# Pacing the row gathers of a fused convolution and expert layer by landings and by matrix steps

## The chip, the cores and the metric

The kernel runs on one core of one Trainium2 chip. A core has five engines with an instruction queue each, which run side by side and wait for one another through semaphores: TensorE (PE; its weight loads are shown apart as PEld), VectorE (DVE), ScalarE (ACT), GpSimd (POOL) and SyncE (SP, which here only starts transfers). Sixteen DMA engines move data between the device's memory and the on-chip buffers. The metric is the device time of one execution in microseconds (us); a version counts by the median of its runs.

## The reference

Two branches act on the same normalised input and are added to it:

```python
def reference(A_q, A_k, A_v, A_shift_k, A_ssm_k, A_ssm_D, B_x, B_w_q, B_k1, B_k2, B_u, B_v):
    ...
        # A: short causal convolution of k, times v, then a long causal convolution
        kv = k_shift * v
        y = irfft(rfft(pad(kv)) * rfft(pad(ssm_k)))[:, :S] + kv * ssm_D
        return q * y
    ...
        # B: each token picks 2 of 4096 experts per head by product keys
        q = jnp.einsum("nd,dhc->nhc", xf, w_q)
        s1 = jnp.einsum("nhd,ed->nhe", q1, k1)
        s2 = jnp.einsum("nhd,ed->nhe", q2, k2)
        i1 = jnp.argsort(-s1, axis=-1)[..., :K]
        i2 = jnp.argsort(-s2, axis=-1)[..., :K]
        ...
        ue = u[top_e]
        ve = v[top_e]
        act = _gelu(jnp.einsum("nd,nhkd->nhk", xf, ue))
        out = jnp.einsum("nhk,nhk,nhkd->nd", g, act, ve)
    ...
    x = A_q
    xn = _layernorm(x, axis=-1)
    return x + _A_ref(xn, A_k, A_v, A_shift_k, A_ssm_k, A_ssm_D) + _B_ref(xn, B_w_q, B_k1, B_k2, B_u, B_v)
```

(The long convolution is written out here in short; the code does it with FFTs.) There are 2048 tokens of 448 channels, 16 heads, and two experts per head, so each token fetches 32 rows. A row of `u` and one of `v` lie side by side in one table, `uv`, and are fetched together.

## The kernel before

The tokens are cut into 16 tiles of 128. The work is a set of streams, written as Python generators that yield operations: an engine, a cost in us, a function that emits the instructions, what it waits for, and what it makes available. A planner (`Planner.run`, L190) plays a list schedule with these costs: it takes the operation that can start first by its own clock, emits its instructions, and goes on. The order of instructions on every engine is the order in which the planner emitted them, and is fixed when the kernel is built. The framework then puts a semaphore wait wherever an instruction needs data or a buffer of another one.

There are three parts in time. First the weights of the scores are folded with the keys (`w_load` to `w_low`; SP loads 16 pieces of `wq`). Then, tile after tile, the scores are made (`s_mm`, PE, L394 to L398), DVE takes the top values of each of 32 groups (`s_top`: eight `max` at L430, and eight `max_index` at L435 in four operations of two), small DVE operations (L462 to L478) choose the two experts per head, PE turns the result round (L506), and ACT writes the row numbers to `idx` and the weights to `gt` (L495). After the last tile's scores their buffers are given back, and the convolution (from `c_in`, L785, to `c_gate`, L904) runs in two halves of channels, with `fm` tables loaded by SP (L809).

The expert streams run beside all of that. A batch is a set of 4 gathers, and there are 128 batches, 512 gathers in all. A gather (L524) is one indirect DMA that POOL issues: it fetches 128 rows of 896 floats, by the row numbers in `idx`, to a quarter of a `uv` buffer. There are 5 such buffers (`NBUF`), of which one is lent to the convolution for some time; a batch takes the buffer that comes free first, so its first gather waits for the value step of the batch that had it. For a batch, PE spreads the tokens (`xr`, L537), DVE multiplies them into the rows (L557 takes two gathers at once, L564 one), ACT sums what L557 left (L576), takes the gelu (L580) and weighs it (L604; DVE at L602 for some), and PE adds up the values (`pv`, L615, the value step that frees the buffer). ACT copies the sums of a tile's quarter (`vs`, L625), PE folds them (L634) and DVE adds them to the output (L636).

POOL issues nothing but gathers, except at the start and for 14 products of the short convolution of the second half (`tap`, L676), which lie between gathers in its queue; DVE adds those at L701. A gather signals its landing on one of eight semaphores in turn, so the framework already makes each gather wait for the landing of the eighth ahead.

Of the kernel before, what the change touches and what calls it, by code (L numbers as in the profile page):

```python
# [33 lines left out]
HOLD = 11  # L34
SHIFT = 2
ON_POOL = (1, 3)


N = 2 * S
# [42 lines left out]
class Ring:  # L82


    def __init__(self, n, banks=None):
        self.n, self.releases, self.banks = n, [], banks
# [51 lines left out]
class Planner:  # L138
# [5 lines left out]
    def __init__(self):  # L144
        self.free = dict.fromkeys(("PE", "DVE", "ACT", "POOL", "SP"), 0.0)
        self.busy = dict(self.free)
        self.done, self.streams, self.dma, self.loads, self.part = {}, [], 0.0, 0.0, 0.5
        self.log = {e: [] for e in self.free}

    def add(self, prio, ops):  # L150
        s = [prio, iter(ops), None]
        self.streams.append(s)
        return s
# [33 lines left out]
    def run(self, until):  # L187
        while any(s in self.streams for s in until):
            for s in list(self.streams):
                if s[2] is None:  # L190
                    s[2] = next(s[1], None)
                    if s[2] is None:
                        self.streams.remove(s)
            heads = {}
            for s in self.streams:
                t = self.start(s[2])
                if t is not None:
                    heads.setdefault(s[2].eng, []).append((t, s[0]() if callable(s[0]) else s[0], s))
            if not heads:
                if any(s in self.streams for s in until):  # L200
                    raise RuntimeError("no operation can go on: " + str([(s[0], s[2].eng, s[2].key, s[2].waits) for s in self.streams]))
                return
            best = None
            for eng, cands in heads.items():
                cands.sort(key=lambda c: (c[0], c[1]))
                pick = cands[0]
                while True:
                    late = [c for c in cands if c[1] < pick[1] and c[0] < pick[0] + pick[2][2].cost - (self.SLIP if pick[1] < 3 else 0.0)]
                    if not late:
                        break  # L210
                    pick = min(late, key=lambda c: (c[1], c[0]))
                if best is None or pick[0] < best[0]:
                    best = pick
            t, _, s = best
            op, s[2] = s[2], None
            op.fn()
            end = t + op.cost
            self.busy[op.eng] += op.cost
            self.log[op.eng].append((t, op.cost))
            self.free[op.eng] = end  # L220
            for r, k in op.rings:
                r.releases.append(k)
                if getattr(r, "banks", None):
                    r.banks.append(k)
            if op.moved:
                end = self.transfer(op, end + 2.0) + 0.6
            if op.key is not None:
                self.done[op.key] = (end + op.lag, op.eng if not op.moved else "DMA")
# [3 lines left out]
def parallel_kernel(ctx, tc, x, wq, kk, uv, cf, cm, h0, kv0, hv1, k1, ca, out):  # L232
    nc = tc.nc
    ctx.enter_context(tc.manual_schedule())
    ap = ctx.enter_context(tc.tile_pool(name="ap", bufs=1))
# [4 lines left out]
    ws_ctx = ExitStack()  # L240
    wp = ws_ctx.enter_context(tc.tile_pool(name="wp", bufs=1))
    plan = Planner()
    r_xr, r_uv, banks = Ring(1), Slots(NBUF, plan), Slots(6, plan)
    r_sc, r_a, r_v, r_z = (Ring(n, banks) for n in CAPS)

# [14 lines left out]
    idx = ap.tile([P, NT, NG], I32, name="idx")  # L260
# [6 lines left out]
    live = {}  # L267
# [151 lines left out]
    def s_top(tiles):  # L419
        for T in tiles:  # L420
            def begin(T=T):
                live["mx", T] = wp.tile([P, 32, 8], F32, tag="mx", bufs=2, name="mx")
                live["mi", T] = wp.tile([P, 32, 8], U32, tag="mi", bufs=2, name="mi")
            for n in range(4):
                def peak(T=T, n=n):
                    live["top"] = T + n / 4
                    if n == 0:
                        begin()
                    for j in range(8):
                        nc.vector.max(live["mx", T][:, 8 * n + j, :], live["sc", T, n][:, 64 * j:64 * j + 64])  # L430
                yield Op("DVE", 1.05, peak, [("sc", T, n)], rings=[(r_mx, ("eg", T))] if n == 0 else [])
                for j in range(0, 8, 2):
                    def find(T=T, n=n, j=j):
                        for k in range(8 * n + j, 8 * n + j + 2):
                            nc.vector.max_index(live["mi", T][:, k, :], live["mx", T][:, k, :], live["sc", T, n][:, 64 * (k % 8):64 * (k % 8) + 64])  # L435
                    yield Op("DVE", 0.4, find, key=("tk", T, n) if j == 6 else None, rings=[(r_mi, ("eg", T))] if n == j == 0 else [])

# [76 lines left out]
    NB = len(order)  # L514
    ends = {(r, j): max(b for b, o in enumerate(order) if o[0] == r and o[2] == j) for r in range(len(rounds)) for j in range(4)}

    def e_gather():
        for b, (r, T, j, hf) in enumerate(order):
            for c in range(4):
                def go(b=b, T=T, g=8 * j + 4 * hf + c, c=c):  # L520
                    if c == 0:
                        live["batch"] = b
                        live["uv", b] = gp.tile([P, 4, 2 * D], F32, tag=f"uv{r_uv.first()}", name="uv")
                    nc.gpsimd.indirect_dma_start(live["uv", b][:, c, :], None, uv, bass.IndirectOffsetOnAxis(ap=idx[:, T, g:g + 1], axis=0))  # L524
                if c == 0 and loan.slot is None and ("y", 0, 0) in plan.done:
                    loan.take()
                yield Op("POOL", 1.25, go, [("idx", T, hf if T == 0 else 0)], key=("land", b, c), moved=4.6e5,
                         rings=[(r_uv, ("v", b))] if c == 0 else [])
# [156 lines left out]
    def t_taps():  # L685
        def by(b, t):
            return ("POOL", 1.1, nc.gpsimd) if t in ON_POOL else ("DVE", 0.62, nc.vector)
        for b in range(NBK):
# [232 lines left out]
    def lead():  # L921
        return -1 if live["top"] < live["batch"] / 8 + AHEAD else 2
    scores = [plan.add(p, s(range(1, NT))) for s, p in ((s_mm, lead), (s_split, lead), (s_top, lead), (s_pairs, lead), (s_gate, -1), (s_place, -1), (s_put, -1))]
    experts = [plan.add(0, s()) for s in (e_gather, e_values, e_weigh, e_share, e_spread, e_dots, e_gelu, e_out, e_fold)]
    plan.run(heads)
    f13, skd = (ap.tile([P, WS], F32, tag="ws", bufs=2, name="cs") for i in range(2))
# [79 lines left out]
```

## Time and profile before

| | us |
|---|---|
| runs | 976.0, 967.79, 976.12 (median 976.0) |
| the profiled execution, device time | 965.93 |
| its span, first to last instruction | 964.1 |
| POOL: median time to issue one gather | 0.946 |

The profiled execution had a mean granted TensorE clock of 0.866 of full speed. The page gives the busy time of each engine, the queues' bytes, the chain of work that ended last (followed back from the last instruction, at each step to what released it) and the groups of instructions by line. A group's row reads: line, engine, operation, output and inputs, count; then busy time and mean duration in ns; then the idle time of the engine just ahead of them, and what ended most of that. In a row of the timeline the first two numbers are start and duration in us, and the bracket gives the idle time ahead and its releaser. "remote", and in the chain "another core or an unknown queue", stand for a wait whose end the profile can put down to no instruction; "issue" is idle time with no releaser at all near its end.

### The profile page before, as it was taken

Reading aid. Unit: us, or ns where it says so; the run is one execution under the profiler, and the core shown is the slowest. Engines: PE = TensorE matmul, PEld = TensorE weight load, DVE = VectorE, ACT = ScalarE, POOL = GpSimd, SP = SyncE. Lnnn points to the kernel's source line nnn. Section 1 sums busy time; section 2 is a strip of 40 time slices with the busy share of each in tenths; the row PEclk is TensorE's granted clock in tenths of the full one; section 3 lists DMA queues with packets and bytes.
Section 4 is the critical chain, followed back from the end, with each engine's and each line's share of the span. In section 5 each row is a group of like instructions: output and inputs, shape, how many; then the busy total and the mean of one; then the engine's idle time right before and its main releaser. Section 6 shows DMA issues by size and latency. Waiting matters only on the chain.

```text
span 964.1 us, 16745 instructions
## 1 busy us (share of the span) xinstructions
PE 748.2 (78%) x5100; PEld 417.0 (43%) x5100; DVE 658.3 (68%) x2559; ACT 589.4 (61%) x1971; POOL 511.0 (53%) x532
## 2 busy tenths in 40 slices
PE   6948668758898798878876776788778885986886
PEld 3425333424454444434433444344436664543454
DVE  4538666867797778968868669887684751673645
ACT  4745665656675666656656757695863662874642
POOL 0063365564565666556665565667673465366530
PEclk9978787878878988879998786999997986998888
DMA  9983588796888978878888998889999588599852
GB/s 380 389 314 124 197 307 304 257 330 211 281 290 297 316 259 304 295 255 304 294 312 302 406 330 314 291 292 391 329 324 386 161 301 297 181 357 360 314 204 87
DMA packets 55338, 280.68 MB, mean 291 GB/s; under 512 B 9425, under 2 KB 13905, under 8 KB 54353
## 3 DMA queue, kind: packets, MB, share of 16 engines
q0 software_dynamic: 40960, 234.91, 69.5%
q1 hardware_dynamic: 13856, 42.43, 11.5%
q10 hardware_dynamic: 432, 2.28, 0.7%
q8 instruction: 41, 0.67, 0.3%
q14 instruction: 49, 0.39, 0.1%
HBM read 275.91 MB, written 3.67 MB: 290 GB/s over the span
## 4 chain that ended last, share of the span: by engine, by line
PE 42%; DVE 19%; ACT 14%; issue 11%; another core or an unknown queue 8%; DMA 4%; POOL 1%; DVEq 0%; ACTq 0%; SPq 0%
PE pv L615 9%; ACT uv L576 6%; DVE uv L557 6%; PE ps L785 5%; DVE mi L435 4%; PE fin L893 4%; PE psx L817 4%; DMA uv<-in_uv_dram,idx 3%; PE sc L394 3%; DVE mx L430 3%; PE psu L849 3%; PE xr L537 3%; PE sc L396 3%; PE sc L395 2%
## 5 line engine op out<-in xcount | busy, mean ns | idle before, releaser
L524 POOL DMA_INDIRECT uv<-in_uv_dram,idx x512 | 494.9, 967 | 405.4 <-issue 129.7
L576 ACT ACTIVATE uv<-uv 128x448 f32<-128x448 f32 x434 | 245.3, 568 | 69.6 <-DVE uv L557 37.2
L557 DVE TENSOR_TENSOR uv<-xr,uv 128x896 f32<-128x896 f32 x217 | 232.1, 1077 | 27.9 <-PE xr L537 15.4
L615 PE MATMUL pv<-uv,cc 128*32 128x448 f32 x1024 | 168.6, 626 | 83.4 <-ACT cc L604 31.4
L435 DVE FIND_INDEX8 mi<-mx,sc 128x8 uint32<-128x64 f32 x512 | 105.1, 219 | 11.6 <-issue 11.5
L394 PE MATMUL sc<-wh,xh 128*128 128x512 f32 x192 | 92.5, 482 | 12.4 <-ACT xh L408 9.1
L615 PEld LDWEIGHTS pv<-uv,cc 128*32 128x32 f32 x1024 | 39.3, 114 | 140.3 <-ACT cc L604 42.4
L785 PE MATMUL ps<-cs,x 128*64 128x132 f32 x896 | 75.5, 320 | 30.0 <-issue 16.7
L430 DVE MAX8 mx<-sc 128x8 f32<-128x64 f32 x512 | 73.1, 211 | 27.6 <-remote 11.9
L396 PE MATMUL sc<-wh,xl 128*128 128x512 f32 x192 | 85.2, 444 | 4.7 <-DVE xl L415 3.6
L395 PE MATMUL sc<-wl,xh 128*128 128x512 f32 x192 | 84.9, 442 | 3.1 <-issue 1.8
L785 PEld LDWEIGHTS ps<-cs,x 128*64 128x64 f32 x896 | 63.7, 160 | 53.3 <-issue 32.1
L576 ACT ACTIVATION_READ_ACCUMULATOR uv<-uv 128x1 f32 x434 | 82.2, 189 | 0.0
L625 ACT ACTIVATE vs<-pv 128x448 f32<-128x448 f32 x68 | 36.6, 538 | 68.1 <-remote 37.1
L834 DVE TENSOR_TENSOR x<-psx,x 128x448 f32<-128x448 f32 x66 | 40.9, 621 | 53.7 <-ACT x L827 38.7
L394 PEld LDWEIGHTS sc<-wh,xh 128*128 128x128 f32 x192 | 41.6, 217 | 68.2 <-issue 32.4
L604 ACT ACTIVATE cc<-fg,ge 128x32 f32<-128x32 f32 x284 | 67.7, 310 | 1.5
L795 ACT ACTIVATE x<-ps 128x396 f32<-128x396 f32 (+1 forms) x84 | 35.7, 461 | 50.9 <-remote 25.3
L849 PE MATMUL psu<-x,fm 128*128 128x224 f32 x248 | 57.2, 371 | 9.2 <-DVE x L834 4.8
L817 PE MATMUL psx<-x,fm 128*128 128x448 f32 x132 | 59.9, 583 | 2.7 <-DMA fm<-in_cm_dram 1.8
L537 PE MATMUL xr<-xn,rep 32*128 32x448 f32 x136 | 50.0, 676 | 15.4 <-DVE uv L557 8.7
L849 PEld LDWEIGHTS psu<-x,fm 128*128 128x128 f32 x248 | 46.1, 195 | 28.5 <-issue 16.5
(100 smaller groups left out, 982.8 us busy)
## 6 DMA issues: line engine op xcount, KB each, us to landing
wq<-in_wq_dram SPq DMA_DIRECT2D x16, 896.0 KB
fm<-in_cm_dram SPq DMA_DIRECT2D x32, 320.0 KB
uv<-in_uv_dram,idx POOLq DMA_INDIRECT x512
x<-in_hv_dram SPq DMA_DIRECT2D x2, 1792.0 KB
acc<-in_x_dram SPq DMA_DIRECT2D x1, 3136.0 KB
x<-in_kv_dram ACTq DMA_DIRECT2D x2, 1048.0 KB
kst<-in_k_dram SPq DMA_DIRECT2D x7, 268.0 KB
out_dram<-acc SPq DMA_DIRECT2D x1, 1344.0 KB
```

The source lines that it names most:

```text
L394: nc.tensor.matmul(sc, xh[:, c, :], wh[:, c, ns], start=(c == 0), stop=False)
L395: nc.tensor.matmul(sc, xh[:, c, :], wl[:, c, ns], start=False, stop=False)
L396: nc.tensor.matmul(sc, xl[:, c, :], wh[:, c, ns], start=False, stop=False)
L430: nc.vector.max(live["mx", T][:, 8 * n + j, :], live["sc", T, n][:, 64 * j:64 * j + 64])
L435: nc.vector.max_index(live["mi", T][:, k, :], live["mx", T][:, k, :], live["sc", T, n][:, 64 * (k % 8):64 * (k % 8) + 64])
L524: nc.gpsimd.indirect_dma_start(live["uv", b][:, c, :], None, uv, bass.IndirectOffsetOnAxis(ap=idx[:, T, g:g + 1], axis=0))
L557: nc.vector.tensor_mul(u, live["xr", r, j][:, None, :D].broadcast_to([P, 2, D]), u)
L576: nc.scalar.activation(u, u, AF.Copy, accum_out=live["act", b][:, c:c + 1])
L615: nc.tensor.matmul(pv[32 * c:32 * c + 32, :D], cc[:, c, :], buf[:, c, D:], start=first, stop=last, tile_position=(0, 32 * c))
L785: nc.tensor.matmul(ps[64 * i:64 * i + 64, w * j:w * j + w], src, f1[:, i, :], start=True, stop=True, tile_position=(0, 64 * i))
L817: nc.tensor.matmul(ps[:, :2 * HALF], live["fm", g, q // 2][:, q % 2, :128], x1[:, :, :, q, :], start=True, stop=True)
L849: nc.tensor.matmul(o, fm[:, k, at:at + 128], y, start=(j == 0), stop=(j == 1))
```

## The change

Two waits are added to gathers, and one order is turned round.

1. From the fifth gather on, each waits for the landing of the fourth ahead of it (`FLY`).
2. The planner keeps a list of its PE steps: the planned end of each and its last instruction. When a gather is planned at `plan.now`, the last step with a planned end of at least 1.5 us earlier (`BEHIND`) is looked up among the last 40, and the gather waits for it, unless the gather named last had the same one.
3. In `s_top`, the searches for the indices of a group of eight go from its last member to its first. The operations, their costs and their places in the plan stay.

```diff
+FLY = 4
+BEHIND = 1.5
+DATA = mybir.DependencyInfo(mybir.DependencyClass.Sync, mybir.DependencyReason.DATA)
...
+        self.now, self.steps, self.last = 0.0, [], None
...
             op, s[2] = s[2], None
+            self.now = t
             op.fn()
             end = t + op.cost
+            if op.eng == "PE":
+                self.steps.append((end, self.last()))
...
     plan = Planner()
+    plan.last = lambda: nc.cur_bb.bb.instructions[-1].name
...
                     def find(T=T, n=n, j=j):
-                        for k in range(8 * n + j, 8 * n + j + 2):
+                        for k in range(8 * n + 7 - j, 8 * n + 5 - j, -1):
                             nc.vector.max_index(live["mi", T][:, k, :], live["mx", T][:, k, :], live["sc", T, n][:, 64 * (k % 8):64 * (k % 8) + 64])
...
+    landed = []
+
     def e_gather():
...
-                    nc.gpsimd.indirect_dma_start(live["uv", b][:, c, :], None, uv, bass.IndirectOffsetOnAxis(ap=idx[:, T, g:g + 1], axis=0))
+                    it = nc.gpsimd.indirect_dma_start(live["uv", b][:, c, :], None, uv, bass.IndirectOffsetOnAxis(ap=idx[:, T, g:g + 1], axis=0))
+                    if len(landed) >= FLY:
+                        tc.add_manual_dep(it.ins, landed[-FLY].ins.name, DATA, reason="gathers on their way")
+                    landed.append(it)
+                    gate = next((name for end, name in reversed(plan.steps[-40:]) if end <= plan.now - BEHIND), None)
+                    if gate is not None and gate != live.get("gate"):
+                        live["gate"] = gate
+                        tc.add_manual_dep(it.ins, gate, DATA, reason="gathers keep step with PE")
```

## The prediction

> **What bounds the kernel now.** I read the page first (busy shares, queues, the chain that ended last), then that chain stage by stage, then two stretches of the timeline.
>
> ```profile
> span 964.1 us, 16745 instructions
> PE 748.2 (78%) x5100; PEld 417.0 (43%) x5100; DVE 658.3 (68%) x2559; ACT 589.4 (61%) x1971; POOL 511.0 (53%) x532
> q0 software_dynamic: 40960, 234.91, 69.5%
> PE 42%; DVE 19%; ACT 14%; issue 11%; another core or an unknown queue 8%; DMA 4%; POOL 1%; DVEq 0%; ACTq 0%; SPq 0%
> L524 POOL DMA_INDIRECT uv<-in_uv_dram,idx x512 | 494.9, 967 | 405.4 <-issue 129.7 <-ACT gt L495 46.4 <-DVE mx L430 45.6
> ```
>
> No engine is full. The gathers move 234.91 MB in 512 calls, 459 KB each, and the chain hardly ever waits for them (DMA 4%). What stands out is 8% "another core or an unknown queue": there is only one core, so these are waits for which the profile finds no releaser just before the wait ended. By stage:
>
> ```profile
> by line: another core or an unknown queue 17.1%; PE pw L346 10.9%; DVE mi L435 9.3%; DVE mx L430 7.4%; issue 6.5%; ACT xn L296 6.3%; DMA wq<-in_wq_dram 4.4%; DVE uv L557 3.9%; DMA uv<-in_uv_dram,idx 3.9%; ACT uv L576 3.7%; PE pt L323 3.3%;
> by line: another core or an unknown queue 11.8%; PE pv L615 10.1%; ACT uv L576 9.8%; PE sc L394 8.3%; DVE uv L557 8.1%; issue 7.8%; PE sc L396 6.7%; PE sc L395 6.4%; DVE mi L435 6.1%; DVE mx L430 4.4%; PE xr L537 4.2%; PE sc L398 3.4%; ACT
> by line: issue 11.7%; ACT uv L576 9.6%; DVE uv L557 9.1%; PE pv L615 9.0%; DMA uv<-in_uv_dram,idx 7.9%; another core or an unknown queue 7.3%; PE ps L785 5.8%; DVE mi L435 4.3%; POOL uv L524 3.9%; DVE tap L676 3.5%; DVE tap L751 2.9%; ACT c
> by line: issue 14.9%; PE fin L893 12.6%; PE ps L785 11.8%; PE psx L817 10.8%; PE pv L615 10.7%; PE psu L849 8.6%; PE psz L873 5.2%; another core or an unknown queue 3.7%; PE xr L537 3.1%; DMA uv<-in_uv_dram,idx 2.1%; DVE x L834 2.0%; ACT uv
> ```
>
> The four rows are the chain in 0 to 136 us, 136 to 425, 425 to 660 and 660 to 964. The unexplained share is 17.1% of 136 = 23 us, 11.8% of 289 = 34 us, 7.3% of 235 = 17 us, 3.7% of 304 = 11 us: 85 us in all. The timeline shows what they are (rows of POOL, PE, DVE and ACT, in order of time):
>
> ```profile
> 119.12 0.94 POOL L524 DMA_INDIRECT uv<-in_uv_dram,idx  x1 [3.49 <-ACT ge L580]
> 124.12 0.50 PE L398 MATMUL sc<-wr,xl 64*128 64x512 f32 x1
> 126.73 0.95 POOL L524 DMA_INDIRECT uv<-in_uv_dram,idx  x1 [0.30 <-issue]
> 127.98 0.95 POOL L524 DMA_INDIRECT uv<-in_uv_dram,idx  x1 [0.30 <-issue]
> 132.99 0.95 POOL L524 DMA_INDIRECT uv<-in_uv_dram,idx  x1 [0.30 <-issue]
> 133.38 1.15 DVE L430 MAX8 mx<-sc 128x8 f32<-128x64 f32 x8 [7.84 <-remote]
> 136.42 0.54 ACT L625 ACTIVATE vs<-pv 128x448 f32<-128x448 f32 x1 [6.37 <-remote]
> ```
>
> POOL issues 12 gathers one behind the other, one per 1.25 us (126.73 to 127.98), which asks for 459 KB / 1.25 = 367 GB/s. The score step that ended at 124.62 is seen by DVE at 133.38, 8.8 us later, with DVE free for 7.84 us of it. ACT sees an earlier value step at 136.42 after 6.37 us idle. So the signal of a finished PE step is held while a burst runs, and comes about when the burst's last gather (132.99 + 0.95 = 133.94) is done. A full DMA alone does not do it:
>
> ```profile
> 8.00:40.00 32.00, 30.81 (x149) 14.58 (x146) 15.79 (x86) 18.73 (x56) 0.00 (x0) 1.00 1.01 422
> 124.00:136.00 12.00, 6.21 (x25) 3.18 (x24) 3.01 (x15) 5.67 (x22) 7.57 (x8) 1.00 0.97 354
> ```
>
> (Columns: stretch, its length, busy of PE, PE loads, DVE, ACT, POOL, clock, DMA share, GB/s.) From 8 to 40 us SP's weight loads fill the DMA at 422 GB/s and PE is busy 30.81 of 32 us; in the burst 354 GB/s of gathers leave PE 6.21 of 12 us.
>
> **The gates on PE steps.** In the plan (which the change leaves as it is: no cost, order or due time is touched) each gather has a last PE step that ends at least 1.5 us ahead of it. I laid that list over this execution. From 136 to 425 us 163 of 180 gathers start before their step has ended, by 3.6 us on the mean over all 180; from 425 to 660 it is 34 of 142, and before 136 us 5 of 44. One burst:
>
> ```profile
> 224.59 0.94 POOL L524 DMA_INDIRECT uv<-in_uv_dram,idx  x1 [9.04 <-DVE mi L435]
> 227.19 0.96 PE L615 MATMUL pv<-uv,cc 128*32 128x448 f32 x8
> 231.02 0.96 PE L615 MATMUL pv<-uv,cc 128*32 128x448 f32 x8
> 233.58 0.95 POOL L524 DMA_INDIRECT uv<-in_uv_dram,idx  x1 [0.30 <-issue]
> 236.01 1.15 DVE L430 MAX8 mx<-sc 128x8 f32<-128x64 f32 x8 [3.40 <-PE px L323]
> 238.47 2.34 PE L615 MATMUL pv<-uv,cc 128*32 128x448 f32 x8 [2.96 <-ACT cc L604]
> ```
>
> These eight gathers run in 9.0 us (224.59 to 233.58). Gated, the first waits for the value step that ends at 228.15 (227.19 + 0.96), the fourth for 231.98, the eighth for 240.81: over 12.6 us, 1.6 us each, or 287 GB/s asked for instead of 367. That burst would not fill the DMA, and DVE's 3.40 us would mostly go. I take 65% of the 34 us of this stage: 22 us. Where the steps have ended in time, as at 119 us, the gate still works once a signal is held: the gather at 127.98 has the score step of 124.62 as its gate, whose signal came at 133.38. It and the four behind it would stop, the burst would end at 127.68 instead of 133.94, and by the distance seen (burst end to release 2.5 us at most: 133.94 to 136.42) all is free by 130.2, 3.2 us of 8.8 earlier. I take 35% of the other stages: 0.35 x (23 + 17 + 11) = 18 us. Bounds for both: nothing, and all 85 us.
>
> What waits behind a gated gather is POOL's own queue: later gathers, and 14 tap products. The users of the gathers are DVE's products (two gathers each, x99 to 400 us):
>
> ```profile
> 0.00:400.00 400.00, 197.93 (x208) 0.85 0.81 285
> 0.00:400.00 400.00, 104.92 (x99) 0.85 0.81 285
> 136.00:425.00 289.00, 170.95 (x180) 0.83 0.84 287
> L701 DVE TENSOR_TENSOR ksh<-ksh,tap 128x512 f32<-128x512 f32 x21 | 16.3, 776 | 3.1 <-POOL tap L676 2.6
> L524 POOLq EVENT_SEMAPHORE  x179: 17/43/11349, 22.5 to 919.4; - x179
> L476 DVE TENSOR_TENSOR eg<-sl,epair 128x16 f32<-128x16 f32 (+1 forms) x17 | 3.0, 174 | 3.2 <-DVE sl L475 2.8
> ```
>
> At 400 us 208 gathers have been issued (first row, POOL L524) and 2 x 99 = 198 used (second row, DVE L557): 10 ahead. At the stage's pace (third row, L524) of 289 us / 180 = 1.61 us that is 16 us of lead. A landing takes 3.7 to 6.4 us (below), so 10 us of cover remain against a delay of 3.6 us: no cost. Without that cover every late microsecond would reach DVE. The taps: DVE already waits 2.6 us for them in all; if each of the 14 is held as long as a gather is on the mean, 3.6 us, that is 50 us at the very most, but most are planned well ahead of their sums, so I take 2 us.
>
> **The landing of the fourth ahead.** Pieces of the chain that run from a gather to its landing, and L524 in three stretches:
>
> ```profile
> 503.06 3.68 DMA uv<-in_uv_dram,idx
> 649.15 6.36 DMA uv<-in_uv_dram,idx
> 709.42 6.30 DMA uv<-in_uv_dram,idx
> 600.00:700.00 100.00, 58.25 (x60) 0.93 0.91 323
> 425.00:660.00 235.00, 139.35 (x142) 0.87 0.88 312
> 660.00:964.00 304.00, 142.52 (x146) 0.88 0.78 282
> ```
>
> A piece runs from the start of the issue, so a gather is on its way 3.7 to 6.4 us, at 1.25 us each three to five together. Four on their way feed one per 0.92 to 1.59 us. From 600 to 700 us 60 gathers go out, one per 1.67 us. So this wait trims bursts only where other loads stretch the landing; I take nothing either way (ends: the whole 11 us after 660 us as a gain, the first rival as a loss).
>
> **Added waits.** A wait that an instruction cannot carry costs POOL's sequencer 43 ns (the semaphore row's median). Some 355 gates change from one gather to the next: 15 us in the queue, hidden by the 405.4 us that POOL idles ahead of gathers; exposed, they cost 15 us. PE, SP and ACT get no new instruction, and no queue's order changes.
>
> **The index searches.** 64 groups of eight: the first search now needs the maximum written just before it. An operation that waits for the one before it loses 3.2 / 17 = 0.19 us (L476's idle time): at most 12 us on DVE, whose chain share is 19%, so 2 us. The seven behind need no wait of their own any more; a gain is bounded by the same 12 us. I take 2 us of cost.
>
> **Sum.** The profiled execution took 965.93 us for a span of 964.1. 965.9 - 22 - 18 + 2 + 2 = 930. The shown runs have a median of 976.0 and reach down to 967.79, so the profiled one lies at their fast end; I keep 930 for the median, 4.7% below 976.0.
>
> **Rivals.**
> Late gathers (slower). After 425 us the limit of four becomes the pace, since POOL now also waits out each landing before it starts the next. If a gather is on its way 7.3 us, 0.95 us (its issue, L524's rows) beyond the longest piece seen, four give one per 1.83 us where 1.67 is used; over the 288 gathers issued after 425 us (142 + 146) that is 46 us, and the gate's 22 us before remain: 966 + 46 - 22 = 990. It decides from 4 x 1.67 = 6.7 us on the mean. For it: 6.36 and 6.30 us beside SP's loads. Against: fewer gathers queued should shorten just that. The Trainium skill, "DMA: Bandwidth & Descriptors", section "Anatomy of one DMA — SWDGE (gpsimd) path", puts such a DMA at some 2.0 us plus its bytes at 436 GB/s, by an estimate 3.05 us for a gather; by it four would give one per 0.76 us and this rival could not be. The trace's 3.68 to 6.36 us do not agree. Chance 0.11.
>
> POOL's work itself holds the others, not its burst (no change). The gathers' 494.9 us on POOL stay, however they are spaced, and the stalls move with them: 965.9 + 4 = 970. For it: DVE stalls too while POOL runs. Against: ACT at 136.42 is held just as long, and the release follows the burst's end. The Trainium skill, "GPSIMD Engine Reference", section "1. Specifications", says that GpSimd shares its SBUF interfaces with VectorE; by that rule alone DVE would suffer, and ACT's row speaks against it. Also here: the gates do not bind as executed, because a faster PE runs ahead of POOL. Chance 0.15.
>
> Nearly all held signals go (much faster). 965.9 - 85 + 4 = 885, since the feedback stops each burst at its start. For it: between bursts signals come at once. Against: the first burst of a stage still has open gates. Chance 0.15.
>
> **Chances and range.** 0.59 for the forecast, whose own range is 905 to 955; 0.15, 0.15 and 0.11 for the others. A measurement of this kernel tells about 1% from no change. Faster by more: 0.59 + 0.15 = 0.74; within: 0.15; slower: 0.11. The range runs from 890, near the all-gone case, to 972, past the no-change case; what is left out is the late-gather case and a little beyond.
>
> **What would show it.** Right: unexplained waits fall from 8% of the chain to about 4.5%, most between 136 and 425 us; gathers in the timeline start 1.5 us or more apart there, with PE as their releaser; GB/s is more even; DVE waits for gather landings no more than now. Wrong: the unexplained share stays (second rival), or DVE's products wait for landings and POOL's idle time ahead of L524 is released by DMA (first rival).

## The result, and the profile after

Four runs of the changed kernel took 929.56 to 935.89 us, median 933.71; the kernel before, timed beside it, had a median of 976.06 us. The ratio is 0.959 (95% interval 0.9537 to 0.9644): 4.1% faster. The profiled execution took 935.89 us.

The page after: span, busy shares and the chain by engine.

```profile
span 934.1 us, 16999 instructions
PE 741.5 (79%) x5100; PEld 411.8 (44%) x5100; DVE 665.9 (71%) x2559; ACT 590.1 (63%) x1971; POOL 511.3 (55%) x532
PE 38%; DVE 17%; DMA 14%; issue 11%; ACT 10%; another core or an unknown queue 7%; POOL 2%; SPq 0%; DVEq 0%; POOLq 0%; ACTq 0%
```

The same work in 30 us less. The unexplained waits are down only from 8% to 7%, and DMA is up from 4% to 14%: one wait went, another came. The chain in 0 to 136, 136 to 425, 425 to 660 and 660 to 934 us (one chain, followed back from the last instruction and cut into stages) tells where:

```profile
by line: another core or an unknown queue 22.1%; DMA acc<-in_x_dram 17.9%; PE pv L632 6.3%; DVE mi L443 6.2%; DVE uv L574 5.3%; DVE mx L438 4.7%; DMA wq<-in_wq_dram 4.5%; ACT uv L593 3.7%; issue 3.6%; DMA uv<-in_uv_dram,idx 3.5%; PE xr L554
by line: issue 11.0%; PE pv L632 10.5%; DMA uv<-in_uv_dram,idx 9.7%; another core or an unknown queue 8.9%; ACT uv L593 8.6%; DVE uv L574 7.2%; PE sc L402 6.7%; PE sc L404 5.3%; PE sc L403 5.2%; DVE mi L443 4.9%; PE sc L406 3.3%; POOL uv L5
by line: issue 13.8%; PE ps L802 11.2%; DVE uv L574 9.2%; PE pv L632 7.9%; ACT uv L593 6.9%; another core or an unknown queue 5.6%; PE psx L834 4.8%; DVE mi L443 4.3%; DVE mx L438 3.2%; DMA fm<-in_cm_dram 3.0%; PE psu L866 2.9%; DVE tap L69
by line: DMA uv<-in_uv_dram,idx 20.4%; issue 11.5%; PE fin L910 11.2%; PE ps L802 7.3%; PE pv L632 7.2%; PE psu L866 7.1%; PE psx L834 6.4%; PE psz L890 5.1%; POOL uv L534 3.1%; ACT uv L593 2.2%; DVE uv L574 2.0%; PE xr L554 1.7%; DVE ksh L
```

In the first stage 28.29 us of the unexplained share are one piece at 31.95 us, while weights load, where the chain of before ran through PE's folding. Such a piece comes and goes with the path that the chain takes there, so a share of the chain has to be read with care. From 136 us on the unexplained share fell from 11.8% of 289 us to 8.9% and from 7.3% of 235 us to 5.6%, and in the last stage it is no longer among the shown lines. But landings of gathers (`DMA uv`) now hold 9.7% of the second stage (28 us) and 20.4% of the last (56 us), which had 2.1% before.

The timeline of POOL at the place where the prediction showed a burst:

```profile
120.38 0.94 POOL L534 DMA_INDIRECT uv<-in_uv_dram,idx  x1 [0.54 <-issue]
122.35 0.94 POOL L534 DMA_INDIRECT uv<-in_uv_dram,idx  x1 [1.03 <-ACT cc L621]
...
128.39 0.94 POOL L534 DMA_INDIRECT uv<-in_uv_dram,idx  x1 [1.15 <-ACT uv L593]
...
134.55 0.94 POOL L534 DMA_INDIRECT uv<-in_uv_dram,idx  x1 [1.20 <-DVE uv L574]
136.35 0.94 POOL L534 DMA_INDIRECT uv<-in_uv_dram,idx  x1 [0.85 <-issue]
137.59 0.95 POOL L534 DMA_INDIRECT uv<-in_uv_dram,idx  x1 [0.30 <-issue]
138.85 0.95 POOL L534 DMA_INDIRECT uv<-in_uv_dram,idx  x1 [0.30 <-issue]
```

Thirteen gathers start between 120.38 and 138.85 us, one per 1.54 us instead of 1.25, with short waits spread among them. The other side is the view of POOL's waits (in all, times, longest), before:

```profile
POOL uv L524 <- DMA uv<-in_uv_dram,idx: 6.1, 6, 2.2
```

and after, followed by DVE's products of before and of after:

```profile
POOL uv L534 <- DMA uv<-in_uv_dram,idx: 64.2, 59, 3.7
POOL uv L534 <- PE pv L632: 27.4, 26, 3.9
```

```profile
L557 DVE TENSOR_TENSOR uv<-xr,uv 128x896 f32<-128x896 f32 x217 | 232.1, 1077 | 27.9 <-PE xr L537 15.4 <-remote 6.4 <-issue 3.6
```

```profile
L574 DVE TENSOR_TENSOR uv<-xr,uv 128x896 f32<-128x896 f32 x217 | 232.9, 1080 | 48.9 <-DMA uv<-in_uv_dram,idx 27.6 <-PE xr L554 9.4 <-remote 5.1
```

POOL waits 64.2 us for landings, ten times as long as before, and DVE's products 27.6 us, which they hardly did before. DVE also waits longer for the `tap` products of POOL, which stand in one queue with the gathers: 2.6 us in all before (the `ksh` row in the prediction), and now

```profile
DVE ksh L718 <- POOL tap L693: 15.5, 5, 4.2
```

So two effects of opposite sign lie in the 4.1%.

### The profile page after: what moved, and what is told of

Its sections match the earlier page's. It is cut to its first block, busy times and chain, and to the rows that moved or that the text cites. A ratio compares the mean times of both kernels' runs of the same rounds, so it can differ in the third digit from the quotient of the medians.

```text
span 934.1 us, 16999 instructions
## 1 busy us (share of the span) xinstructions
PE 741.5 (79%) x5100; PEld 411.8 (44%) x5100; DVE 665.9 (71%) x2559; ACT 590.1 (63%) x1971; POOL 511.3 (55%) x532
## 4 chain that ended last, share of the span: by engine, by line
PE 38%; DVE 17%; DMA 14%; issue 11%; ACT 10%; another core or an unknown queue 7%; POOL 2%; SPq 0%; DVEq 0%; POOLq 0%; ACTq 0%
DMA uv<-in_uv_dram,idx 10%; PE pv L632 8%; DVE uv L574 6%; ACT uv L593 6%; PE ps L802 5%; DVE mi L443 4%; PE fin L910 3%; PE psx L834 3%; PE sc L402 3%; PE psu L866 3%; DMA acc<-in_x_dram 3%; PE sc L404 2%; PE sc L403 2%; DVE mx L438 2%
## 5 line engine op out<-in xcount | busy, mean ns | idle before, releaser
L574 DVE TENSOR_TENSOR uv<-xr,uv 128x896 f32<-128x896 f32 x217 | 232.9, 1080 | 48.9 <-DMA uv<-in_uv_dram,idx 27.6
L802 PE MATMUL ps<-cs,x 128*64 128x132 f32 x896 | 72.2, 312 | 23.0 <-ACT uv L593 7.6
L802 PEld LDWEIGHTS ps<-cs,x 128*64 128x64 f32 x896 | 60.0, 156 | 45.2 <-issue 17.4
L834 PE MATMUL psx<-x,fm 128*128 128x448 f32 x132 | 64.0, 617 | 10.3 <-issue 5.5
L866 PEld LDWEIGHTS psu<-x,fm 128*128 128x128 f32 x248 | 47.2, 200 | 28.5 <-DVE x L851 13.9
L581 DVE SCALAR_TENSOR_TENSOR uv<-xr,uv 128x448 f32<-128x448 f32 x78 | 47.0, 617 | 10.2 <-DMA uv<-in_uv_dram,idx 8.8
```

The source lines that it names most:

```text
L574: nc.vector.tensor_mul(u, live["xr", r, j][:, None, :D].broadcast_to([P, 2, D]), u)
L802: nc.tensor.matmul(ps[64 * i:64 * i + 64, w * j:w * j + w], src, f1[:, i, :], start=True, stop=True, tile_position=(0, 64 * i))
L834: nc.tensor.matmul(ps[:, :2 * HALF], live["fm", g, q // 2][:, q % 2, :128], x1[:, :, :, q, :], start=True, stop=True)
L866: nc.tensor.matmul(o, fm[:, k, at:at + 128], y, start=(j == 0), stop=(j == 1))
```

## The experiments

All ratios are to the kernel before on the same chip, in three rounds. The first four runs take the change apart. Theory A there: the gates on PE steps carry the gain. B: the limit of four does. C: the order of the index searches does.

### Gates alone

The changed kernel without the landing wait and with the old order of searches.

```diff
-                    if len(landed) >= FLY:
-                        tc.add_manual_dep(it.ins, landed[-FLY].ins.name, DATA, reason="gathers on their way")
...
-                        for k in range(8 * n + 7 - j, 8 * n + 5 - j, -1):
+                        for k in range(8 * n + j, 8 * n + j + 2):
```

> Only the waits on PE steps are added to the kernel before. Theory A (a held signal stops further gathers, so the gates end bursts early and carry the gain): ratio to the kernel before 0.965 to 0.975, unexplained waits down to about 5% of the chain. Theory B (the limit of four gathers on their way carries the gain): 0.99 to 1.00, unexplained waits stay near 8%. Theory C (the order of the index searches carries it): 0.995 to 1.005.

Measured: 893.26 us, ratio 0.9292 (0.9189 to 0.9396), much faster than the whole change, and twice the gain that theory A had put down. Its chain by engine, and its first three stages (0 to 136, 136 to 425, 425 to 660 us):

```profile
PE 46%; DVE 21%; issue 12%; ACT 9%; DMA 7%; another core or an unknown queue 3%; POOL 1%; SPq 0%; ACTq 0%; DVEq 0%; POOLq 0%
```

```profile
by line: PE pw L354 10.7%; PE pv L630 9.1%; issue 7.5%; ACT xn L304 6.3%; PE sc L402 6.1%; PE sc L403 5.9%; another core or an unknown queue 5.4%; PE sc L404 5.4%; DMA wq<-in_wq_dram 4.4%; DVE mx L438 3.7%; DVE mi L443 3.6%; ACT uv L591 3.5
by line: issue 14.7%; DVE uv L572 13.5%; DVE mi L443 10.4%; PE pv L630 8.4%; PE sc L402 7.1%; DVE mx L438 6.8%; PE sc L404 6.1%; PE sc L403 5.7%; another core or an unknown queue 3.6%; PE sc L406 3.5%; PE xr L552 3.2%; DMA uv<-in_uv_dram,id
by line: issue 13.6%; PE pv L630 10.1%; DMA fm<-in_cm_dram 9.7%; PE ps L800 8.8%; DVE uv L572 7.0%; ACT uv L591 6.5%; DVE mi L443 5.1%; PE psx L832 3.4%; another core or an unknown queue 3.2%; PE psu L864 3.0%; DMA uv<-in_uv_dram,idx 2.7%; 
```

The unexplained shares fall to 5.4, 3.6 and 3.2% (before: 17.1, 11.8 and 7.3). The waits of ACT and DVE that no instruction ends, of before and then with gates alone, are the cleaner measure, since they don't depend on where the chain runs (two of their rows):

```profile
ACT vs L625 <- remote: 37.1, 11, 6.4
DVE mx L430 <- remote: 11.9, 2, 7.8
```

```profile
ACT vs L640 <- remote: 9.1, 7, 2.9
DVE mx L438 <- remote: 5.4, 2, 2.7
```

Summed over the whole trace and all engines but POOL, such waits come to some 197 us before, 75 with the whole change and 49 with gates alone (a stall of PE can count twice there, once for its weight load).

When the gain comes can be read from the start of equal gathers, here the 289th and the last of 512, before:

```profile
528.35 0.94 POOL L524 DMA_INDIRECT uv<-in_uv_dram,idx  x1 [2.06 <-remote]
...
926.94 0.94 POOL L524 DMA_INDIRECT uv<-in_uv_dram,idx  x1 [0.30 <-issue]
```

and, with gates alone, the 33rd and these two:

```profile
104.03 0.94 POOL L534 DMA_INDIRECT uv<-in_uv_dram,idx  x1 [3.63 <-ACT ge L595]
...
499.82 0.95 POOL L534 DMA_INDIRECT uv<-in_uv_dram,idx  x1 [0.30 <-issue]
...
869.92 0.95 POOL L534 DMA_INDIRECT uv<-in_uv_dram,idx  x1 [0.30 <-issue]
```

The 33rd gather of before is the one at 119.12 us in the prediction's fence. So 15.1 us are won before the 33rd gather, 13.4 more up to the 289th (528.35 - 499.82 = 28.5), and 28.5 from there to the last (57.0). The span is 67.3 us shorter (964.1 to 896.8), so 10 come behind the last gather. These are single executions; in two kernels below with the same gates, one without the landing wait and one with six ahead, the stretch from the 33rd gather to the 289th takes 392 and 395 us (here 395.8, before 409.2).

### The landing wait alone, the searches alone, and both without the landing wait

```diff
+                    if len(landed) >= FLY:
+                        tc.add_manual_dep(it.ins, landed[-FLY].ins.name, DATA, reason="gathers on their way")
```

> Only the wait for the landing of the fourth gather ahead is added. Theory A: ratio 0.99 to 1.005, since only a fifth of the gathers would have waited and a burst of four on their way still fills the DMA. Theory B: 0.96 to 0.97, unexplained waits down to about 5% of the chain. Theory C: 0.995 to 1.005.

Measured: 926.89 us, ratio 0.9695 (0.9583 to 0.9807). That is theory B's number and not A's. Alone, the limit of four is a gain too: it also breaks bursts, and the waits that no instruction ends (all but POOL's) come to 108 us.

> Only the index searches run from the last head to the first. Theories A and B: ratio 0.995 to 1.005 (at most 2 us of cost). Theory C (fewer waits and signals of DVE on itself): 0.97 to 0.98.

Only the order of the searches turned round: 963.68 us, ratio 1.0037 (0.9997 to 1.0077). Theory C falls.

> The whole change without the wait for the fourth landing (gates and index order stay). Theory A: ratio 0.96 to 0.97, as the whole change, or a little better in the convolution, where the landing wait has entered the chain (DMA 10% of it). Theory B: 0.985 or above.

The changed kernel without the landing wait: 893.27 us, ratio 0.9308 (0.9194 to 0.9423), as gates alone, and not the 0.96 to 0.97 that was expected. (Its chain has 7% unexplained all the same, of which a piece of 29.96 us at 31.27 us is 3, as in the changed kernel; the waits that no instruction ends, but POOL's, come to 81 us.) So the gates give 7% and the landing wait beside them takes 3% back, though by itself it gives 3%. The gains don't add, since both come from the same bursts; the cost of the wait remains.

### Where the landing wait costs, and why

Four kernels with gates, and the landing wait in part of the kernel or with six in place of four; in the last one the gates stop at the 289th gather.

```diff
-                    if len(landed) >= FLY:
+                    if len(landed) >= 288:
```

> The gates on all gathers, and the wait for the landing of the fourth ahead only from the 289th gather on (about 500 us into the execution). Theory D: what the landing wait costs beside the gates, it costs in the convolution, where the table loads share the DMA and every late landing reaches VectorE; so this is as slow as the whole change: ratio to before 0.95 to 0.965. Theory E: the landing wait costs by its own handling in POOL's queue, evenly over the 512 gathers: with 224 of the 508 waits, 0.93 + 0.44 x 0.03 = 0.943.

```diff
-                    if len(landed) >= FLY:
+                    if FLY <= len(landed) < 288:
```

> The gates on all gathers, and the landing wait only up to the 288th gather. Theory D: nothing beside the gates alone, 0.925 to 0.935, since there the gathers of all paced versions were issued at the same times. Theory E: 0.93 + 0.56 x 0.03 = 0.947.

```diff
-FLY = 4
+FLY = 6
```

> The gates, and a wait for the landing of the sixth ahead in place of the fourth; the number of waits is nearly the same. Theory D (too few on the way at once is what costs): six hardly bind, 0.925 to 0.94. Theory E (the handling of an added wait): as the whole change, 0.955 to 0.965.

```diff
-                    if gate is not None and gate != live.get("gate"):
+                    if gate is not None and gate != live.get("gate") and len(landed) <= 288:
```

> No landing wait, and gates on the first 288 gathers only. By the issue times of gather 288 (528.4 us before, 499.8 us with all gates) 29 us of the 67 us would be there and the rest lost again: ratio 0.96 to 0.97. If what the gates gain is all in the score stage and the later gain is only its consequence: 0.93 to 0.94. If the early gates only move the wait: 0.98 to 1.0.

| gates | landing wait | ratio (95%) | GB/s from 460 us to the end |
|---|---|---|---|
| all | none | 0.9292 (0.9189 to 0.9396) | 325 |
| all | first 288 | 0.9251 (0.9199 to 0.9302) | 318 |
| all | all, of the sixth ahead | 0.927 (0.9215 to 0.9325) | 320 |
| all | from the 289th on | 0.9572 (0.9512 to 0.9633) | 300 |
| all | all (the change, with the searches) | 0.959 (0.9537 to 0.9644) | 300 |
| first 288 | none | 0.9643 (0.9586 to 0.9699) | 294 |

The kernel before moves 297 GB/s there. The wait costs nothing before the 289th gather and the whole 3% from there on, in the convolution: side by side, 936.05 us with it in the later part, 903.59 with it in the earlier and 903.36 with six ahead. It isn't the handling of an added wait (theory E): with six ahead there are as many waits, and no cost. Theory D stands as to the place, and as to too few on the way at once. The last row says that gates on the first 288 gathers keep 3.6 of 7.1%: the gates work in both halves.

One thing that happens in the convolution shows best where SP issues loads in a row. The timeline of the changed kernel, SP first, then POOL and one product of DVE:

```profile
705.40 0.33 SPq L826 DMA_DIRECT2D fm<-in_cm_dram  x1
706.30 0.80 SPq L735 DMA_DIRECT2D x<-in_hv_dram  x2
```

```profile
716.27 0.94 POOL L534 DMA_INDIRECT uv<-in_uv_dram,idx  x1 [4.55 <-PE psz L890]
...
719.82 0.94 POOL L534 DMA_INDIRECT uv<-in_uv_dram,idx  x1 [2.61 <-DMA uv<-in_uv_dram,idx]
...
723.04 1.09 DVE L574 TENSOR_TENSOR uv<-xr,uv 128x896 f32<-128x896 f32 x1 [3.88 <-DMA uv<-in_uv_dram,idx]
723.71 0.94 POOL L534 DMA_INDIRECT uv<-in_uv_dram,idx  x1 [2.94 <-DMA uv<-in_uv_dram,idx]
```

and two pieces of its chain:

```profile
709.52 13.43 DMA uv<-in_uv_dram,idx
...
835.79 7.24 DMA uv<-in_uv_dram,idx
```

A gather issued just behind these loads is 13.43 us on its way. POOL may not send the fourth behind it until that landing, starts one per 3.5 to 3.9 us (716.27, 719.82, 723.71), and DVE stands for 3.88 us.

But most of the loss lies elsewhere. Equal gathers take equal time from the 289th to the 311th (34.9 us, and 36.3 with gates alone). From the 311th to the 391st the changed kernel needs 147.1 us and gates alone 131.3, so 16 of the 28 us that it loses between the 289th and the last gather lie there; some 5 lie from there to the 421st, the gathers above among them, and 9 behind it. The stretch of these 80 gathers, changed kernel, then gates alone (columns: stretch, length, busy of the gathers on POOL with their count, clock, DMA share, GB/s):

```profile
545.00:692.00 147.00, 81.81 (x80) 0.86 0.87 300
```

```profile
536.00:667.00 131.00, 81.43 (x80) 0.92 0.93 334
```

The DMA is less full there with the landing wait, not fuller, and the granted clock of TensorE is lower too. Four of DVE's five waits for `tap` products, 12.1 of the 15.5 us, lie in it, between 620 and 686 us: a gather that waits for a landing holds the product behind it in POOL's queue, and so the convolution. The kernel with the wait from the 289th gather on has this on its chain:

```profile
656.13 8.29 DMA uv<-in_uv_dram,idx
...
666.18 1.08 POOL tap L693
...
667.28 0.04 DVE ksh L718
```

In all, DVE waits 15.5 us for taps with the whole change, 22.5 with the landing wait from the 289th on and 13.4 with it alone, but 1.7 with gates alone, 4.0 with the wait on the first 288 and 3.5 with six ahead. So the products held in POOL's queue are likely a good part of the loss. How much of the 27 to 29 us they are (0.9572 and 0.959 less 0.9292, of 965.9) stays open: no run took them out of POOL's queue.

A second reading is that a short queue of gathers gets a smaller share of a full DMA. In 24 us from the start of a group of SP's loads, changed kernel, then gates alone (columns as above):

```profile
490.00:514.00 24.00, 10.40 (x11) 0.64 0.99 385
```

```profile
488.00:512.00 24.00, 14.64 (x16) 0.75 0.98 388
```

The DMA is full either way and moves the same (385 and 388 GB/s), but POOL starts 11 gathers against 15 (the 16 count one that began before), and the gathers' queue moves 4.62 MB in place of 5.82, SP's 4.58 in place of 3.47. The Trainium skill, "DMA: Bandwidth & Descriptors", section "SWDGE vs HWDGE vs iDMA", says that each DMA engine takes turns between its queues, and that gathers from GpSimd and loads from SP are in different ones. The rows fit that; that the short queue runs empty between its turns isn't shown. Nor is this what the wait costs in the end: these are the gathers from the 281st on, and the kernel with the wait on the first 288 takes 18.1 us from the 281st to the 289th (the changed kernel 20.2, gates alone 11.1) and is no slower in all.

### What holds the signals, and how close a gate must be

Six memsets on POOL behind each fourth gather, in the kernel before; no wait is added.

```diff
+    rest = ap.tile([P, 64], F32, name="rest")
...
                     nc.gpsimd.indirect_dma_start(live["uv", b][:, c, :], None, uv, bass.IndirectOffsetOnAxis(ap=idx[:, T, g:g + 1], axis=0))
+                    if c == 3:
+                        for _ in range(6):
+                            nc.gpsimd.memset(rest, 0.0)
```

> The kernel before, with six small memsets on POOL (estimate from the memset rows, 1.0 to 1.4 us together) behind each fourth gather, and no wait added: a burst is spread to some 1.55 us a gather, 296 GB/s, whatever PE does. Theory A (a burst near what the DMA can move holds the signals, any gap lets them through): the unexplained waits fall as with the gates, 0.93 to 0.96. Theory G (the gate works because it waits for the very signal that is held): a blind pause does little, 0.98 to 1.01. Theory P (POOL's work holds the others): more POOL work, over 1.01.

Measured: 954.23 us, ratio 0.9808 (0.9743 to 0.9874). By its time that is theory G's number; by its waits it is A. The chain by engine, two groups, and two waits of ACT:

```profile
PE 29%; DMA 17%; issue 17%; POOL 16%; DVE 13%; ACT 7%; another core or an unknown queue 1%; SPq 0%; POOLq 0%; DVEq 0%; ACTq 0%
L561 DVE TENSOR_TENSOR uv<-xr,uv 128x896 f32<-128x896 f32 x217 | 234.6, 1086 | 130.6 <-DMA uv<-in_uv_dram,idx 112.5
```

```profile
L528 POOL MEMSET rest<- 128x64 f32 x768 | 119.0, 155 | 36.7
```

```profile
ACT zt L884 <- remote: 25.8, 8, 5.1
ACT vs L629 <- remote: 1.1, 1, 1.1
```

A blind pause takes most of the unexplained waits away, with 119.0 us more work on POOL: 1% of the chain is left, ACT's wait for the value sums goes from 37.1 to 1.1 us, and DVE's at the scores isn't listed any more. Others stay, as ACT's at `zt` (10.6 us before), and all but POOL's come to 51 us, as with gates alone. That speaks against theory P. The time hardly follows, because POOL is now the bound: POOL and DMA hold 33% of the chain, DVE's products wait 112.5 us for landings, and 25.7 us go for taps. A pause that comes whether it is needed or not is paid in pace.

Next, the same bytes without POOL: direct loads of consecutive table rows, issued by SP.

```diff
-                    nc.gpsimd.indirect_dma_start(live["uv", b][:, c, :], None, uv, bass.IndirectOffsetOnAxis(ap=idx[:, T, g:g + 1], axis=0))
+                    nc.sync.dma_start(live["uv", b][:, c, :], uv[128 * ((4 * b + c) % 32):128 * ((4 * b + c) % 32) + 128, :])
```

> The kernel before, with each gather replaced by a direct load of 128 rows that lie one behind the other in the table, of the same bytes to the same place, issued by SP; it leaves out the choice of the rows, and POOL issues nothing in the batches. Theory A as I hold it (the hold belongs to gathers that POOL issues): the unexplained share of the chain between 136 and 425 us falls from 11.8% to under 4% though the bytes are the same. Theory V (a DMA that is asked for more than it moves holds signals, whoever issues): it stays at 8% or more. The time alone tells little, since SP's own loads now stand in one queue with these.

Measured: 780.32 us, ratio 0.8008 (0.795 to 0.8067). The chain by engine, and the stage from 136 to 425 us (busy of PE, PE loads, DVE, ACT, POOL, then clock, DMA share, GB/s):

```profile
PE 41%; DVE 28%; ACT 13%; DMA 11%; issue 5%; SPq 1%; DVEq 0%; ACTq 0%
```

```profile
136.00:425.00 289.00, 257.20 (x1555) 136.79 (x1555) 279.99 (x1510) 231.35 (x846) 0.00 (x0) 0.93 0.98 367
```

Not one unexplained wait is left, in the chain or in the list of waits, at 367 GB/s over the whole stage, as much as the bursts asked for. Theory V falls: here a DMA full of direct loads holds no signals. The experiment takes away three things together, POOL's part, the software queue and the scattered rows; which of them holds the signals stays open. Its time is no measure of the hold, since these loads also don't wait for the row numbers: the first starts at 33.3 us, where the first gather of before starts at 47.7.

Last, the gates alone at other distances from the plan.

```diff
-BEHIND = 1.5
+BEHIND = 0.0
```

> Gates alone, with each gather waiting for the last PE step that the plan ends at or ahead of it (0 in place of 1.5 us). Were the lead of the gathers (about 16 us) enough for any gate, 0.92 to 0.935; did later gathers reach VectorE, 0.95 to 0.98.

```diff
-BEHIND = 1.5
+BEHIND = 5.0
```

> Gates alone, 5 us behind the plan. If a gate only has to stop a burst once a signal is held for several us, most of the gain stays: 0.93 to 0.945. If gathers must keep close step with PE, about half is lost: 0.955 to 0.975.

Measured: 0.9334 (0.9263 to 0.9406) at 0, 0.9292 at 1.5, 0.958 (0.9518 to 0.9642) at 5. Between 0 and 1.5 there is no difference clear of the noise; at 5 us some 40% of the gain is lost. The waits that no instruction ends (all but POOL's) go the same way: 56, 49 and 128 us. So a gate has to act before a signal has been held for long, and up to 1.5 us closer to PE no cost of later gathers shows.

## Why the prediction was right, and where it was not

The time was right: 930 predicted, 933.7 measured. But two parts of the sum were wrong, with opposite signs, and nearly cancelled: that the number was so close is luck.

- **What bounds the kernel: right.** The unexplained waits are signals held while POOL sends bursts of gathers. Breaking the bursts takes most of them away, with gates or with blind pauses, and moving the bytes without POOL takes all.
- **The gates: the mechanism right, the size too small.** I took 22 us between 136 and 425 us and 18 elsewhere, 40 in all. Measured, 0.0708 x 965.9 = 68 us (58 to 78 by its interval). The 18 were the mis-sized part: to the 33rd gather 15.1 us were won where 35% of 23 gives 8, and behind the 289th, gates alone win 38.8 us (67.3 - 28.5) where 35% of 17 and 11 gives 10. The share of the chain was no bound there. A reading, not a measurement: a held signal also delays the next gathers and table loads, which then meet other work, and those pieces are booked elsewhere. From the 33rd gather up to the 289th 13.4 us were won, less than the 22. (The burst by which I sized that term is also misread: from its first gated gather to its eighth, 12.66 us hold seven steps, 1.8 us each and not 1.6.)
- **The landing of the fourth ahead, and the taps: the steps that failed.** I took nothing for the landing, because four gathers on their way 3.7 to 6.4 us feed one per 0.92 to 1.59 us, faster than they go out, and 2 us for the taps. Together with the gates the wait costs 27 to 29 us, all in the convolution, and DVE alone waits 15.5 us for taps. I asked for the taps what a gate would do to them, and not what a landing would. My first rival had the place (behind 425 us), and with 46 us it had the sign, but its condition wasn't met: counted from the packets of the gathers' queue (80 to a gather, in the order of their ends), the gathers from the 289th on take 5.0 us on the mean from issue to last packet, and the 15 such pieces of its chain run about 1 us longer on the mean; 6.7 would have decided. Only 15 of the 224 take longer than 6.7, the longest 12.4. So it isn't the mean but the late ones, and what stands behind them in POOL's queue. The Trainium skill's page "DMA: Bandwidth & Descriptors", in the section "Anatomy of one DMA — SWDGE (gpsimd) path", led to an estimate of 3.05 us and no such cost; the pieces of 7.24 and 13.43 us and the ratio of 0.9572 against 0.9292 decide against it.
- **Added waits: small, as taken.** With six ahead there are as many waits on POOL, and the ratio stays at 0.927. The changed kernel has 254 instructions more (16999 against 16745), where I priced some 355.
- **The searches: right.** 2 us of cost taken, 0.0037 x 965.9 = 3.6 us measured, with an interval from about nothing to 7 us.
- **No change, and all signals gone.** The rival by which POOL's work itself holds the others fell to the pauses. The one by which nearly all held signals go, 885 us, has about the number of the gates alone (893), but a quarter of those waits is left there (49 of 197 us).
- **The signs I named.** Gathers 1.5 us apart: yes at the burst shown (1.54), but PE released none of the gathers in its rows; over the whole kernel its value steps ended 27.4 us of their waits. Unexplained waits at 4.5% of the chain: 7%, of which the one piece of 28.29 us at the start is 3. GB/s more even: yes, the page's 40 slices, the last one apart, fell to 124, 161 and 181 before and not under 246 after. DVE waiting for landings no more than now: no, and that row was named as the first rival's sign.

## What to carry to other kernels

Where POOL sends indirect gathers back to back, look for waits with no releaser that end with the burst, and pace the gathers by steps of the consumer that end shortly ahead of them. Don't also cap the transfers in flight so low that one slow landing stops the queue: here four cost 3% and six nothing, though the mean landing would have allowed four. Ask what else stands in the queue that the cap holds, here the tap products. When two edits are aimed at the same waits, run each alone: here the gates without the landing wait (893 us) beat both kernels.

## What the runs showed of the hardware beyond that

- The granted clock of TensorE rose with the pacing. For the same 5100 matmuls PE was busy 748.2 us before (clock 0.866), and with gates alone and with direct loads:

```profile
PE 714.6 (80%) x5100; PEld 402.5 (45%) x5100; DVE 661.5 (74%) x2559; ACT 590.6 (66%) x1971; POOL 514.5 (57%) x532
```

```profile
PE 676.4 (87%) x5100; PEld 383.0 (49%) x5100; DVE 648.5 (83%) x2559; ACT 587.9 (75%) x1971; POOL 15.7 (2%) x20
```

The mean clocks are 0.897 and 0.933. So part of the gates' 68 us comes as shorter matmuls, and that may be why the convolution gained more than its held signals were worth. Whether the clock is a cause or follows from the steadier work isn't settled: the kernel with the landing wait from the 289th gather on also has 0.896 in its profiled execution, at 938 us (0.880 to 0.885 in its other three).
- Fetching chosen rows by POOL costs this kernel more than their bytes: loading as many bytes directly, without waiting for the row numbers, takes a fifth off its time, with the DMA at 0.98 of its time busy from 136 to 425 us.
